# A banded-attention and gated-MLP kernel on one core: four weight sums open at once, the first batch's global queries moved to the end, values turned by VectorE and DMA

## The chip, the cores and the metric

One Trainium2 chip, one of its cores. The metric is device microseconds for one execution, median of the runs. The kernel before takes 809.63 us (three runs, 809.60 to 809.93).

## The reference

Eight batches of eight heads, 512 local and 32 global tokens each, head size 64. Global queries attend to all 544 keys; a local query attends to the 32 global keys and to local keys at most 32 positions away. The 4608 token vectors (512 wide) then go through a gated layer without a nonlinearity:

```python
s_g   = scale * q_g @ [k_g, k_l].T          # 32 x 544 per head
out_g = softmax(s_g) @ [v_g, v_l]
s_ll  = where(|i - j| <= 32, scale * q_l @ k_l.T, -1e9)
out_l = softmax([scale * q_l @ k_g.T, s_ll]) @ [v_g, v_l]
x = [out_g, out_l] as 4608 x 512
a, b = x @ w1, x @ w2                       # 512 x 1024 each
h = (a * b) @ w3                            # 1024 x 1024
result = h @ w_out                          # 1024 x 512
```

All four weight matrices arrive as 8-byte floats.

## The kernel before, in words

**Units of work.** A pair `m` (0 to 31) is two heads of one batch, four pairs to a batch; a quad `u` (0 to 15) is two pairs' global queries. A quarter `k` (0 to 16) of the gated layer takes 256 tokens: two per batch, and quarter 15 takes the 256 global tokens. The weights `w3` and `w_out` are multiplied first on the chip: the product `w34` is made in eight sums `t` of eight matmuls `fold(t, j)`, which need `w3` block (t, j // 4) and `w_out` block j. `first(k, m, c)` is 12 matmuls of x with a block of w1 (c = 0) or w2 (c = 1); `second(k, m)` multiplies the gated block with `w34` block m. Numbers are kept as a high part and a low part, so each product is three matmuls.

**A pair in steps** (names as in the order lists): loads `q`, `k`, `v`; `kc` and `vc` spread global keys and values into K and V; `s` scores on TensorE into a PSUM bank; `mm` and `ex` subtract the maximum and take exponentials, with row sums in `sm`; from pair TP = 4 on `tn` transposes blocks of 32x32 on VectorE, `po` writes them to DRAM in four DMAs and `pi` reads them back (pairs below 4 use TensorE transposes `tp` and copies `pt`); `v` values on TensorE; `iv` the reciprocal of the sums; `nm` normalizes on VectorE into `vo`; `xt` (line 396) four TensorE transposes of 128x128 into a PSUM bank; `xh` and `xl` split the result into x. K has two buffers, V three; V is filled by five DMAs a pair, since its rows are kept at three shifts.

**Global queries.** `sg` (line 427) 32 small matmuls per pair, `gm` maximum, then per quad `gr`, `ge` (exponentials), `gt` (VectorE transpose), `go` (four DMAs out), `gi` (in), `vg` values, `gn`, `gb` (one transpose), `gc`, `gd` (DMA to `xg`). At the end `gin`, `gxh`, `gxl` read `xg` for quarter 15. Each batch's global queries run beside its pairs.

**Weights.** `fetch` loads a 512 KB block into one of three raw buffers; `unit` steps 0, 2, 3 unpack it (VectorE, ScalarE, VectorE), steps 4 and 5 split a block of w1 and w2 into high and low. Blocks of w1 and w2 with m of 4 and more (`w12s`, 16 pieces of 256 KB through three buffers) are written where the blocks of `w3` and `w_out` lay, so their steps 4 and 5 wait for all eight sums and for the split of the other w1 and w2 blocks.

**Order.** Nothing is scheduled by the program: `ORDER_OF` holds, for each kind of step, its place in one global order, with a letter (A, D, P) where an engine is chosen, and each engine executes its steps in that order. SyncE (SP) issues every DMA. `ORDER` gives the order of the weight blocks, `W3F` the tiles that hold unpacked `w3` blocks. In `take(tag, bufs, ...)` a step that opens a tile waits for the readers of the tile that used the buffer before.

Of the kernel before, what the change touches and what calls it, by code (L numbers as in the profile page):

```python
# [35 lines left out]

ORDER_OF = dict(
    load="0 50 51 59 45 48 70 73 85 133 136 139 200 201 368 259 263 387 229 232 346 362 647 443 463 664 522 509 753  "
# [19 lines left out]
    "323 328 332 367 375 386 391",
    w34h="A105 D102 A155 A227 A298 A284 A359 A397",
    w34l="107 104 157 231 301 287 364 407",  # L60
    vc="A62 P65 D71 A64 A67 D75 A369 A372 P371 A377 A650 P648 P654 A660 A751 D752 P755 A754 A915 D917 P919 A918  "
    "A1016 P1015 A1018 P1020 A1183 D1185 P1187 A1186 A1284 P1283 A1286 P1288 A1451 D1453 P1455 A1454 A1552 P1551  "
    "A1554 P1556 A1719 D1721 P1723 A1722 A1820 P1819 A1822 P1824 A1987 D1989 P1991 A1990 A2088 P2087 A2090 P2092  "
    "A2252 D2254 P2256 A2255 A2345 P2346",
    kc="A72 P74 D121 A120 P186 A187 P239 P245 P322 D326 P390 P405 P500 D503 P532 A530 P705 P710 D728 P730 D807 A808  "
    "D867 P870 A960 P961 A995 P996 D1075 A1076 D1135 P1138 A1228 P1229 A1263 P1264 D1343 A1344 D1403 P1406 A1496  "
    "P1497 A1531 P1532 D1613 A1614 D1671 P1674 A1764 P1765 A1799 P1800 D1881 A1882 D1939 P1942 A2032 P2033 A2067  "
    "P2068 D2147 A2148 D2205 P2208",
    s="76 130 226 299 379 467 601 688 764 824 886 957 1032 1092 1154 1225 1300 1362 1422 1493 1568 1630 1690 1761  "
# [29 lines left out]
    iv="116 166 265 336 449 569 663 721 802 857 925 991 1067 1126 1193 1259 1335 1394 1461 1527 1603 1662 1729 1795  "
    "1873 1930 1997 2063 2139 2196 2262 2323",  # L100
    nm="160 198 294 414 499 681 733 787 834 941 988 1043 1104 1209 1256 1311 1372 1477 1524 1579 1640 1745 1792  "
    "1847 1908 2013 2060 2115 2174 2277 2320 2362",
    xt="165 203 297 419 508 682 736 794 839 942 997 1048 1109 1210 1265 1316 1377 1478 1533 1584 1645 1746 1801  "
    "1854 1913 2014 2069 2120 2179 2278 2327 2364",
# [90 lines left out]
def band_attention_glu_kernel(  # L195
# [484 lines left out]
    def pair(m):  # L680
# [74 lines left out]
        if m % 2 == 0:  # L755
            return
# [230 lines left out]
```

## Time and profile before

| | |
|---|---|
| median of 3 runs | 809.63 us |
| the profiled execution | 808.85 us, span 807.1 us |
| granted TensorE clock, mean | 0.985 |
| TensorE matmul busy | 96% of the span |
| VectorE, ScalarE, GpSimd busy | 51%, 40%, 7% |
| DMA moved | 121.30 MB, 150 GB/s |

The span runs from the first to the last instruction; the rest of the execution's time lies around it. Busy is the time in which an engine had an instruction in work. Matmuls overlap in the pipeline, so one matmul's duration is longer than the step from its start to the next one's start; costs of TensorE work are read from differences of starts. "fp32" matmuls appear as more than one record in some forms. A wait is put down to what ended it.

### The profile page before, as it was taken

Reading aid. Unit: us, or ns where it says so; the run is one execution under the profiler, and the core shown is the slowest. Engines: PE = TensorE matmul, PEld = TensorE weight load, DVE = VectorE, ACT = ScalarE, POOL = GpSimd, SP = SyncE. Lnnn points to the kernel's source line nnn. Section 1 sums busy time; section 2 is a strip of 40 time slices with the busy share of each in tenths; the row PEclk is TensorE's granted clock in tenths of the full one; section 3 lists DMA queues with packets and bytes.
Section 4 is the critical chain, followed back from the end, with each engine's and each line's share of the span. In section 5 each row is a group of like instructions: output and inputs, shape, how many; then the busy total and the mean of one; then the engine's idle time right before and its main releaser. Section 6 shows DMA issues by size and latency. Waiting matters only on the chain.

```text
span 807.1 us, 25268 instructions
## 1 busy us (share of the span) xinstructions
PE 777.9 (96%) x10676; PEld 670.9 (83%) x10676; DVE 413.0 (51%) x1333; ACT 324.0 (40%) x970; POOL 55.2 (7%) x88
## 2 busy tenths in 40 slices
PE   6699887999999999999999999999999999999998
PEld 3255486888988999998988999999899999999997
DVE  3666787756454545454554455545554645231121
ACT  3665744534343534353434334533453334111111
POOL 1000221100000100010001000100010000000000
PEclk9899999899999999999999999999999999999999
DMA  6987686477347634773375537563566353310000
GB/s 217 297 241 255 193 240 196 127 211 202 101 120 198 188 113 116 200 201 121 106 208 152 160 107 193 145 192 110 157 170 173 111 146 112 108 41 27 1 27 27
DMA packets 76489, 121.30 MB, mean 150 GB/s; under 512 B 13272, under 2 KB 41560, under 8 KB 76376
## 3 DMA queue, kind: packets, MB, share of 16 engines
q1 hardware_dynamic: 76376, 119.69, 51.1%
q8 instruction: 84, 1.38, 0.8%
q14 instruction: 29, 0.24, 0.1%
HBM read 87.15 MB, written 32.51 MB: 148 GB/s over the span
## 4 chain that ended last, share of the span: by engine, by line
PE 89%; DVE 4%; DMA 3%; ACT 2%; issue 1%; SPq 0%; DVEq 0%; ACTq 0%
PE acc L538 8%; PE bp L508 8%; PE acc L540 8%; PE acc L539 8%; PE ap L508 8%; PE bp L510 7%; PE bp L509 7%; PE ap L509 7%; PE ap L510 7%; PE w L645 5%; PE s L329 4%; PE v L379 4%; PE sg L427 2%; PE gx L462 2%; PE xt L396 2%; DMA raw_wo<-in_wo_t_dram 1%
## 5 line engine op out<-in xcount | busy, mean ns | idle before, releaser
L508 PE MATMUL bp<-x,w12h 128*128 128x256 f32 x512 | 148.4, 290 | 5.3 <-DVE gl__1520 L402 3.4
L508 PE MATMUL ap<-x,w12h 128*128 128x256 f32 x512 | 145.2, 284 | 2.5 <-DVE w12h L399 1.9
L510 PE MATMUL bp<-x,w12l 128*128 128x256 f32 x512 | 143.2, 280 | 0.9 <-issue 0.9
L510 PE MATMUL ap<-x,w12l 128*128 128x256 f32 x512 | 143.2, 280 | 0.6 <-POOL w12l L402 0.6
L509 PE MATMUL ap<-x,w12h 128*128 128x256 f32 x512 | 142.9, 279 | 0.6 <-DVE x L402 0.6
L509 PE MATMUL bp<-x,w12h 128*128 128x256 f32 x512 | 143.1, 280 | 0.0
L341 ACT ACTIVATE P<-P,mn 128x128 f32<-128x128 f32 x256 | 99.8, 392 | 27.5 <-DVE mn L336 26.7
L508 PEld LDWEIGHTS bp<-x,w12h 128*128 128x128 f32 x512 | 97.1, 190 | 10.4 <-issue 9.0
L508 PEld LDWEIGHTS ap<-x,w12h 128*128 128x128 f32 x512 | 96.7, 189 | 5.8 <-DVE w12h L399 2.1
L509 PEld LDWEIGHTS ap<-x,w12h 128*128 128x128 f32 x512 | 96.8, 189 | 3.2 <-DVE x L402 0.9
L510 PEld LDWEIGHTS bp<-x,w12l 128*128 128x128 f32 x512 | 97.7, 191 | 1.2 <-issue 1.1
L510 PEld LDWEIGHTS ap<-x,w12l 128*128 128x128 f32 x512 | 97.2, 190 | 1.2 <-POOL w12l L402 1.0
L509 PEld LDWEIGHTS bp<-x,w12h 128*128 128x128 f32 x512 | 97.4, 190 | 0.0
L336 DVE CUSTOM_DVE_ANT_0 P<-s,cs 128x128 f32<-128x128 f32 x256 | 58.8, 285 | 66.3 <-PE s L329 60.7
L645 PE MATMUL w<-wo,w3f 128*128 128x512 f32 x128 | 63.7, 635 | 10.8 <-DVE wo L569 7.5
L645 PEld LDWEIGHTS w<-wo,w3f 128*128 128x128 f32 x128 | 23.6, 199 | 40.4 <-issue 21.6
L341 ACT ACTIVATION_READ_ACCUMULATOR P<-P,mn 128x1 f32 x256 | 48.2, 188 | 0.0
L305 POOL COPY K<-K 128x480 f32<-128x480 f32 x28 | 16.8, 603 | 399.5 <-DMA K<-in_kp_t_dram 378.5
L545 ACT COPY o<-acc 128x512 f32<-128x512 f32 x34 | 20.0, 587 | 52.6 <-PE acc L540 51.1
L295 ACT COPY V<-vg 32x1024 f32<-32x1024 f32 x33 | 33.7, 1045 | 16.1 <-PE gx L465 15.9
L399 ACT CAST x<-xt 128x256 fp32r<-128x256 f32 x50 | 17.6, 373 | 55.0 <-PE xt L396 53.5
L379 PEld LDWEIGHTS v<-V,Pt 128*32 128x32 f32 x2048 | 30.2, 110 | 10.1 <-issue 4.1
(780 smaller groups left out, 1408.3 us busy)
## 6 DMA issues: line engine op xcount, KB each, us to landing
Pd<-P SPq DMA_DIRECT2D x112, 128.0 KB, 2.9
Pt<-Pd SPq DMA_DIRECT2D x28, 512.0 KB, 3.4
raw_w<-in_w_t_dram SPq DMA_DIRECT2D x24, 512.0 KB, 5.4
V<-in_v_t_dram SPq DMA_DIRECT2D x64, 192.0 KB, 4.5
K<-in_kp_t_dram SPq DMA_DIRECT2D x32, 272.0 KB, 3.2
out_dram<-o SPq DMA_DIRECT2D x34, 256.0 KB, 2.3
q<-in_q_t_dram SPq DMA_DIRECT2D x32, 256.0 KB, 3.7
V<-in_v_t_dram SPq DMA_DIRECT2D x32, 256.0 KB, 4.0
```

Of the source, the lines that this page charges most:

```text
L295: (nc.scalar.copy if eng is nc.scalar else eng.tensor_copy)(to, src)
L329: nc.tensor.matmul(block(st[:, h], x, 128 * g), q[64 * h : 64 * h + 64, c : c + 32], window(m, h, 4 * g + x), start=True, stop=True, skip_ ...
L336: nc.vector.tensor_tensor_reduce(T["P", m][:, :, h, g], chunks(T["s", m][:, h, 128 * g : 128 * g + 128]), chunks(masks[g]), -0.125, 3.0e38 ...
L341: nc.scalar.activation(P, P, AF.Exp, bias=T["mn", m][:, g, h : h + 1], scale=-1.0, accum_out=T["sm", m][:, g, h : h + 1])
L379: nc.tensor.matmul(vt[32 * x : 32 * x + 32, g, h], t[:, x, h, g], Vs[m % NV][:, x, h, g], start=True, stop=True, skip_group_check=True)
L508: nc.tensor.matmul(d, wh[:, k, c, :], x[:, 0, 0:w], start=(k == m % 2 == 0), stop=False, skip_group_check=True)
L509: nc.tensor.matmul(d, wh[:, k, c, :], x[:, 1, 0:w], start=False, stop=False, skip_group_check=True)
L510: nc.tensor.matmul(d, wl[:, k, c, :], x[:, 0, 0:w], start=False, stop=(k == 3), skip_group_check=True)
L538: nc.tensor.matmul(a, gh[:, m % 2, sl], wh, start=(m == 0), stop=False)
L539: nc.tensor.matmul(a, gh[:, m % 2, sl], wl, start=False, stop=False)
L540: nc.tensor.matmul(a, gl[:, m % 2, sl], wh, start=False, stop=(m == 7))
L645: nc.tensor.matmul(T["w34", t], T["w3f", t, j // 4][:, j % 4], T["wo"][:, j], start=(j == 0), stop=(j == 7))
```

## The change

What it does, part by part:

1. Weights: the blocks of `w3` for t = 0 to 3 come first, and four sums are open at once, two in the banks `acc` and one each in `a` and `b`. The unpacked `w3` blocks get more tiles (`x1` too, of which there are 6 in place of 7).
2. The first batch's global queries: batch 0's `sg` to `gd` leave the place beside its pairs and follow those of the last batch, as quads 16 and 17. K, V and the global values of batch 0 are loaded and spread again for them.
3. `VC` = 4: for pairs 0 to 3, V is loaded by one DMA, and four copies by an engine (`vs`) make the shifted rows.
4. Values from pair 4 on: `xt` is replaced by `vn` (VectorE transpose of 32x32 blocks), `vw` (four DMAs to DRAM) and `vi` (one DMA back into an SBUF tile `xr`, two buffers). `vo` has one buffer in place of two, `sm` two in place of three; the reciprocals go to a tile `si`. `xl` and `xh` may run on GpSimd. Tokens in x lie in another order, and `store` writes rows accordingly.
5. `sg` of two pairs in one step, so both K buffers are read by it.
6. All places in `ORDER_OF` are new.

```diff
-NX, NO, MA = (4, 7), 3, 4
+NX, NO, MA = (4, 6), 3, 4
+NXR, NVO = 2, 1
-LAG, TP = 1, 4
+LAG, TP, LATE, VC = 1, 4, 4, 4
 ORDER = (
-    ('w3', 0, 0), ('wo', 0, 0), ('w3', 1, 0), ('wo', 1, 0), ('wo', 2, 0), ('wo', 3, 0), ('w3', 0, 1), ('wo', 4, 0),
-    ('w3', 1, 1), ('wo', 5, 0), ('wo', 6, 0), ('wo', 7, 0), *[('w3', t, e) for t in range(2, 8) for e in range(2)],
+    ('w3', 0, 0), ('wo', 0, 0), ('w3', 1, 0), ('w3', 2, 0), ('w3', 3, 0), ('wo', 1, 0), ('wo', 2, 0), ('wo', 3, 0),
+    ('w3', 0, 1), ('wo', 4, 0), ('w3', 1, 1), ('w3', 2, 1), ('w3', 3, 1), ('wo', 5, 0), ('wo', 6, 0), ('wo', 7, 0),
...
-W3F = ("w3f", "w3f", "g", "as", "gh", "gl")
+W3F = ("w3f", "w3f", "g", "as", "gh", "gl", "x1", "x1", "w3f", "w3f", "g", "as", "gh", "gl", "w3f", "w3f")
+SUMS = ("acc", "acc", "a", "b", "acc", "acc", "acc", "acc")
...
         nc.sync.dma_start(V[32:64], src)
+        if m < VC:
+            return
...
+    def shift_v(m, part, eng):
+        V = Vs[m % NV]
+        if part < 2:
+            to, src = V[64 * part : 64 * part + 32, 1 - part : 4 - part], V[32:64, part : part + 3]
+        else:
+            x = 3 * (part - 2)
+            to, src = V[64 * (part - 2) :][0:32, x, :, 3 - part : 6 - part], V[32:64, 3 - x, :, part - 2 : part + 1]
+        (nc.scalar.copy if eng is nc.scalar else eng.tensor_copy)(to, src)
...
+    def values_turn(m):
+        vo = T["vo", m].rearrange("p g c d -> p c g d").rearrange("p c g d -> p (c g d)")
+        nc.vector.transpose(vo, vo)
+
+    def values_out(m):
+        vo = T.pop(("vo", m)).rearrange("p g c d -> p c (g d)")
+        d = T["vd", m] = dram.tile([128, 4, 128], F32, tag="vd", name=f"vd{m}", bufs=3)
+        for x in range(4):
+            nc.sync.dma_start(d[:, x].rearrange("(c j) q -> j c q", c=4), vo[32 * x : 32 * x + 32])
+
+    def values_in(m):
+        T["x", m] = p2.tile([128, 512], F32, tag="xr", name=f"xr{m}", bufs=NXR)
+        nc.sync.dma_start(T["x", m], T.pop(("vd", m)).rearrange("p x c -> p (x c)"))
...
-            T["w34", t] = ps_acc.tile([128, 512], F32, tag="acc", name=f"w34_{t}")
+            T["w34", t] = (ps_acc if SUMS[t] == "acc" else ps_1).tile([128, 512], F32, tag=SUMS[t], name=f"w34_{t}")
...
-        take("x", 1, ("x", m), ("xt", m))
-        add(("xt", m), "PE", [("nm", m), ("load", "cs")], back, m)
+        if m < TP:
+            take("x", 1, ("x", m), ("xt", m))
+            add(("xt", m), "PE", [("nm", m), ("load", "cs")], back, m)
+        else:
+            add(("vn", m), "DVE", [("nm", m)], values_turn, m)
+            add(("vw", m), "SP", [("vn", m)], values_out, m)
+            add(("vi", m), "SP", [("vw", m)], values_in, m)
...
-        add(("sg", m), "PE", [("load", "qg", b), *kc], g_scores, m)
+        add(("sg", u), "PE", [("load", "qg", b), *[("kc", m - x, y) for x in range(2) for y in range(2)]], g_scores, u)
...
-    for m in range(NM):
-        pair(m)
-        if m >= LAG and (m - LAG) % 2:
+    for m in range(NM + LATE):
+        if m < NM:
+            pair(m)
+        if m >= LATE:
+            global_pair(m)
+        if m >= LATE + LAG and (m - LAG) % 2:
             quad((m - LAG) // 2)
```

Some places in the two order lists of TensorE, read from `ORDER_OF` (steps between the named ones are left out at "..."):

```
before: ... fold(0,7) tp(0,0) sg(0) fold(2,0) ... fold(7,7) v(3) xt(3) first(0,0,0) first(0,1,0) first(0,0,1) first(0,1,1) first(0,2,0) sg(4) ...
after:  ... fold(4,0) ... fold(5,7) s(4) tp(3,0) tp(3,1) v(3) xt(3) first(0,0,0) first(0,1,0) fold(7,0) ... fold(7,7) first(0,0,1) first(0,1,1) ...
after:  ... v(18) first(7,1,1) second(6,6) first(7,2,0) second(6,7) first(7,3,0) v(19) ...
after:  ... sg(8) first(6,0,1) first(6,1,1) second(5,6) first(6,2,0) second(5,7) first(6,3,0) v(17) first(6,2,1) first(6,3,1) second(6,0) first(6,4,0) second(6,1) first(6,5,0) s(18) ...
```

## Rows read from the trace of the kernel before

**Rows 1.** The page's first part: busy us, share of span, instructions of each engine.

```profile
span 807.1 us, 25268 instructions
PE 777.9 (96%) x10676; PEld 670.9 (83%) x10676; DVE 413.0 (51%) x1333; ACT 324.0 (40%) x970; POOL 55.2 (7%) x88
```

**Rows 2.** Stretches: length, busy us per engine, granted clock, DMA share, GB/s.

```profile
0.00:40.00 40.00, 27.29 (x155) 13.23 (x156) 21.31 (x53) 18.32 (x37) 5.31 (x26) 0.87 0.83 257
40.00:96.00 56.00, 55.88 (x750) 29.40 (x749) 37.55 (x138) 33.50 (x97) 5.35 (x7) 1.00 0.74 228
96.00:156.00 60.00, 48.25 (x576) 41.80 (x575) 48.76 (x149) 29.56 (x98) 12.75 (x17) 0.89 0.69 196
156.00:700.00 544.00, 542.89 (x8463) 489.80 (x8466) 282.56 (x958) 225.79 (x713) 31.76 (x39) 1.00 0.54 154
700.00:803.50 103.50, 103.50 (x757) 96.70 (x745) 22.87 (x40) 16.25 (x28) 0.00 (x0) 1.00 0.07 22
```

**Rows 3.** Waits of TensorE in 0 to 160: total us, times, longest.

```profile
PE w L645 <- DVE wo L569: 7.5, 5, 3.9
PE bp L508 <- DVE gl__1520 L402: 3.4, 1, 3.4
```

**Rows 4.** Timeline of TensorE: start us, us, instruction; around one `xt`.

```profile
262.59 0.28 PE L510 MATMUL ap<-x,w12l 128*128 128x256 f32 x1
262.70 0.60 PE L396 MATMUL xt<-cs,vo 128*128 128x128 f32 x4
263.06 0.37 PE L508 MATMUL ap<-x,w12h 128*128 128x256 f32 x1
263.26 0.28 PE L509 MATMUL ap<-x,w12h 128*128 128x256 f32 x1
```

**Rows 5.** Timeline of TensorE: folds, one `sg`, two `first`, two `second`.

```profile
44.05 3.70 PE L645 MATMUL w<-wo,w3f 128*128 128x512 f32 x8
218.02 0.67 PE L427 MATMUL sg<-K,qg 64*32 64x128 f32 x32
218.62 0.51 PE L538 MATMUL acc<-w34h,gh__2651 128*128 128x512 f32 x1
222.87 0.28 PE L508 MATMUL bp<-x,w12h 128*128 128x256 f32 x1
225.59 0.39 PE L538 MATMUL acc<-w34h,gh__2851 128*128 128x512 f32 x1
228.34 0.28 PE L508 MATMUL ap<-x,w12h 128*128 128x256 f32 x1
```

**Rows 6.** Splits of the `w12s` pieces: durations ns, first and last start us.

```profile
L402 DVE TENSOR_TENSOR w12l<-raw_w12s,w12h x12: 410/425/970, 117.6 to 150.3; 128x256 fp32r<-128x256 f32 x12
```

**Rows 7.** DMA issues: count, KB each, median us to landing.

```profile
Pd<-P SPq DMA_DIRECT2D x112, 128.0 KB, 2.9
raw_w<-in_w_t_dram SPq DMA_DIRECT2D x24, 512.0 KB, 5.4
K<-in_kp_t_dram SPq DMA_DIRECT2D x32, 272.0 KB, 3.2
```

**Rows 8.** Groups by form: busy us, mean ns, idle before.

```profile
L349 DVE STREAM_TRANSPOSE P<-P 128x1024 f32<-128x1024 f32 x28 | 34.7, 1238 | 0.2
L389 DVE TENSOR_TENSOR vo<-v,sm 128x512 f32<-128x512 f32 x32 | 21.9, 683 | 11.2 <-PE v L379 11.2
L402 POOL TENSOR_TENSOR w12l<-raw_w12s,w12h 128x256 fp32r<-128x256 f32 x4 | 3.1, 775 | 6.2 <-DVE w12h L399 5.0 <-ACT w12h L399 1.0
L295 ACT COPY V<-vg 32x1024 f32<-32x1024 f32 x33 | 33.7, 1045 | 16.1 <-PE gx L465 15.9
```

**Rows 9.** Timeline of the SP queue around one pair's `po` and `pi`.

```profile
386.96 1.90 SPq L355 DMA_DIRECT2D Pd<-P  x4
391.45 0.34 SPq L360 DMA_DIRECT2D Pt<-Pd  x1
```

More of the change, by code (lines that the diff above doesn't have):

```diff
@@ L58 @@
[L58 to L69, printed above, removed]
@@ L99 @@
[L99 to L104, printed above, removed]
@@ new lines @@
+    gn="667 781 897 1036 1174 1311 1449 1587 1726 1859 1997 2135 2273 2415 2451 2480",
+    gb="677 787 901 1042 1182 1319 1455 1593 1730 1868 2003 2144 2277 2419 2454 2481",
+    gc="D681 A790 D903 D1044 A1184 A1321 D1458 D1595 D1732 D1870 D2006 D2146 D2279 D2422 A2456 D2484",
+    gd="684 795 904 1045 1186 1326 1460 1597 1734 1872 2008 2148 2281 2423 2458 2485",
+    gin="2490 2494 2499 2506",
+    gxh="D2495 D2501 D2507 D2513",
+    gxl="D2496 D2502 D2509 D2514",
+    first="391 397 433 441 444 454 460 477 499 535 514 543 599 629 606 634 637 643 651 661 679 688 702 705 714 721 732  "
[12 rows of a table added]
@@ L415, in convert, with g_scores @@
         split_x((b, p, e), f"x{e}", NX[e], T["x", m][:, 256 * e : 256 * e + 256], 256, part, eng)
-    def g_scores(m):
-        st = T["sg", m] = ps_1.tile([128, 2, 512], F32, tag="s", name=f"sg{m}")
-        u, odd = divmod(m, 2)
-        if not odd:
-            T["G", u] = p2.tile([128, 4, 4, 2, 32], F32, tag="G", name=f"G{u}", bufs=NG)
-            T["mg", u] = p2.tile([128, 4], F32, tag="mg", name=f"mg{u}")
-        for g in range(2):
-            for x in range(4):
-                for h in range(2):
-                    to = st[32 * x : 32 * x + 32, h, 0:256].rearrange("p (a b g j) -> p g a b j", a=2, b=2, g=2)[:, g]
-                    nc.tensor.matmul(to, T["qg", m // NP][64 * h : 64 * h + 64, m % NP],
-                                     window(m, h, 2 * (4 * g + x) + 1).rearrange("p a (b j) -> p a b j", b=2), start=True, stop=True, skip_group_check=True)
+    def g_scores(u):
+        st = T["sg", u] = ps_1.tile([128, 2, 512], F32, tag="s", name=f"sg{u}")
+        T["G", u] = p2.tile([128, 4, 4, 2, 32], F32, tag="G", name=f"G{u}", bufs=NG)
+        T["mg", u] = p2.tile([128, 4], F32, tag="mg", name=f"mg{u}")
+        for m in (2 * u, 2 * u + 1):
+            for g in range(2):
+                for x in range(4):
+                    for h in range(2):
+                        to = st[32 * x : 32 * x + 32, h].rearrange("p (o a b g j) -> p o g a b j", o=2, a=2, b=2, g=2)
+                        nc.tensor.matmul(to[:, m % 2, g], T["qg", m // NP][64 * h : 64 * h + 64, m % NP],
+                                         window(m, h, 2 * (4 * g + x) + 1).rearrange("p a (b j) -> p a b j", b=2),
+                                         start=True, stop=True, skip_group_check=True)
     def g_minus_max(m, h):
@@ L632, in unit @@
                 if kind == "w3" or e % 2 == 0:
-                    tag = W3F[[u[1:] for u in ORDER if u[0] == "w3"].index((a, h)) % len(W3F)]
-                    pool, n = (P["early"], 2) if tag == "w3f" else (p1, 1)
+                    tag = W3F[[u[1:] for u in ORDER if u[0] == "w3"].index((a, h))]
+                    pool, n = dict(w3f=(P["early"], 2), x1=(p1, NX[1])).get(tag, (p1, 1))
                     T["w3f", a, h] = pool.tile([128, 4, 128], F32, tag=tag, name=f"w3f{a}_{h}", bufs=n)
@@ L678, in read, with keys @@
             tiles[name].append(key)
-    def pair(m):
-        b, u = m // NP, m // 2
-        take("q", NQ, ("q", m), ("load", "q", m))
+    def keys(m):
+        b = m // NP
         take("K", NK, ("K", m), ("load", "k", m))
         take("V", NV, ("V", m), ("load", "v", m))
-        for k, fn in (("q", load_q), ("k", load_k), ("v", load_v)):
+        for k, fn in (("k", load_k), ("v", load_v)):
             add(("load", k, m), "SP", (), fn, m)
         if m % NP == 0:
-            take("qg", 2, ("qg", b), ("load", "qg", b))
-            add(("load", "qg", b), "SP", (), load_qg, b)
+            if m >= LATE:
+                take("qg", 2, ("qg", b), ("load", "qg", b))
+                add(("load", "qg", b), "SP", (), load_qg, b)
             take("vg", 4, ("vg", b), ("load", "vg", b))
@@ L696, in pair, with v_ready @@
                 late.append((("vc", m, h), tiles["V", m - NV]))
-        vc = [("vc", m, 0), ("vc", m, 1)]
+        for part in range(4 * (m < VC)):
+            add(("vs", m, part), "POOL ACT DVE", [("load", "v", m)], shift_v, m, part)
+            read(("vs", m, part), ("V", m))
         for part in range(2):
             add(("kc", m, part), "POOL ACT DVE", [("load", "k", m), ("clear", 1)], spread_k, m, part)
+    def v_ready(m):
+        return [("vc", m, 0), ("vc", m, 1), ("load", "v", m), ("clear", 2), *[("vs", m, x) for x in range(4 * (m < VC))]]
+    def pair(m):
+        b = m // NP
+        take("q", NQ, ("q", m), ("load", "q", m))
+        add(("load", "q", m), "SP", (), load_q, m)
+        keys(m)
         kc = [("kc", m, 0), ("kc", m, 1)]
@@ L702, in pair @@
         take("mn", 2, ("mn", m), ("s", m))
-        take("sm", 3, ("sm", m), ("s", m))
+        take("sm", 2, ("sm", m), ("s", m))
         take("P", 2, ("P", m), ("s", m))
@@ L728, in pair @@
         take("v", 1, ("v", m), ("v", m))
-        add(("v", m), "PE", [("pt", m, 0), ("pt", m, 1), *vc, ("load", "v", m), ("clear", 2)] if m < TP else [("pi", m), *vc, ("load", "v", m), ("clear", 2)], values, m)
+        add(("v", m), "PE", [*([("pt", m, 0), ("pt", m, 1)] if m < TP else [("pi", m)]), *v_ready(m)], values, m)
         read(("v", m), ("Pt", m), ("V", m))
         add(("iv", m), "DVE", ex, inverse, m)
-        take("vo", 2, ("vo", m), ("nm", m))
+        read(("iv", m), ("sm", m))
+        take("si", 1, ("si", m), ("iv", m))
+        read(("nm", m), ("si", m))
+        take("vo", NVO, ("vo", m), ("nm", m))
         add(("nm", m), "DVE", [("v", m), ("iv", m)], normalize, m)
-        read(("nm", m), ("v", m), ("sm", m))
-        take("x", 1, ("x", m), ("xt", m))
-        add(("xt", m), "PE", [("nm", m), ("load", "cs")], back, m)
-        read(("xt", m), ("vo", m))
+        read(("nm", m), ("v", m))
+        on = "ACT DVE POOL"
+        if m < TP:
+            take("x", 1, ("x", m), ("xt", m))
+            add(("xt", m), "PE", [("nm", m), ("load", "cs")], back, m)
+            read(("xt", m), ("vo", m))
+            on, src = "ACT DVE", ("xt", m)
+        else:
+            add(("vn", m), "DVE", [("nm", m)], values_turn, m)
+            take("vd", 3, ("vd", m), ("vw", m))
+            add(("vw", m), "SP", [("vn", m)], values_out, m)
+            read(("vw", m), ("vo", m))
+            take("xr", NXR, ("x", m), ("vi", m))
+            add(("vi", m), "SP", [("vw", m)], values_in, m)
+            read(("vi", m), ("vd", m))
+            src = ("vi", m)
         for e in range(2):
@@ L740, in pair, with global_pair @@
             take(f"x{e}", NX[e], x, ("xh", m, e))
-            add(("xh", m, e), "ACT DVE", [("xt", m)], convert, m, e, 0)
-            add(("xl", m, e), "DVE", [("xh", m, e)], convert, m, e, 1)
+            add(("xh", m, e), on, [src], convert, m, e, 0)
+            add(("xl", m, e), "DVE" if m < TP else "DVE POOL", [("xh", m, e)], convert, m, e, 1)
             read(("xh", m, e), ("x", m))
             read(("xl", m, e), ("x", m), x)
-        take("s", 1, ("sg", m), ("sg", m))
-        if m % 2 == 0:
-            take("G", NG, ("G", u), ("sg", m))
-            take("mg", 2, ("mg", u), ("sg", m))
-        add(("sg", m), "PE", [("load", "qg", b), *kc], g_scores, m)
-        read(("sg", m), ("qg", b), ("K", m))
-        for h in range(2):
-            add(("gm", m, h), "DVE", [("sg", m), ("edges",), *[("sg", m - 1)] * (m % 2)], g_minus_max, m, h)
-            read(("gm", m, h), ("sg", m))
+    def global_pair(m):
+        b, u = m // NP, m // 2
+        if m >= NM:
+            keys(m)
         if m % 2 == 0:
             return
+        take("s", 1, ("sg", u), ("sg", u))
+        take("G", NG, ("G", u), ("sg", u))
+        take("mg", 2, ("mg", u), ("sg", u))
+        add(("sg", u), "PE", [("load", "qg", b), *[("kc", m - x, y) for x in range(2) for y in range(2)]], g_scores, u)
+        read(("sg", u), ("qg", b), ("K", m - 1), ("K", m))
+        for x in range(1, -1, -1):
+            for h in range(2):
+                add(("gm", m - x, h), "DVE", [("sg", u), ("edges",)], g_minus_max, m - x, h)
+                read(("gm", m - x, h), ("sg", u))
         gm = [("gm", m - x, h) for x in range(2) for h in range(2)]
@@ L773, in quad @@
         take("x", 1, ("o", u), ("vg", u))
-        add(("vg", u), "PE", [("gi", u), ("edges",), *[(k, 2 * u + x, h) for x in range(2) for k in ("vc",) for h in range(2)],
-                              *[("load", "v", 2 * u + x) for x in range(2)]], g_values, u)
+        add(("vg", u), "PE", [("gi", u), ("edges",), *v_ready(2 * u), *v_ready(2 * u + 1)], g_values, u)
         read(("vg", u), ("Gt", u), ("V", 2 * u), ("V", 2 * u + 1), ("lg", u))
-        add(("gn", u), "DVE", [("vg", u), *([("gb", u - 1)] if u else [("warm",)])], g_normalize, u)
+        add(("gn", u), "DVE", [("vg", u), *([("gb", u - 1)] if 2 * u > LATE else [("warm",)])], g_normalize, u)
         add(("gb", u), "PE", [("gn", u)], g_back, u)
@@ L858, in weight @@
         if kind == "w3":
-            tag = W3F[[x[1:] for x in ORDER if x[0] == "w3"].index((a, e)) % len(W3F)]
-            take(tag, W3F.count(tag), ("w3f", a, e), me[3])
+            tag = W3F[[x[1:] for x in ORDER if x[0] == "w3"].index((a, e))]
+            take(tag, dict(w3f=2, x1=NX[1]).get(tag, 1), ("w3f", a, e), me[3])
         if kind[:3] == "w12":
@@ L868, in product @@
     def product(t):
-        take("acc", 2, ("w34", t), ("fold", t, 0))
+        take(SUMS[t], 2 if SUMS[t] == "acc" else 1, ("w34", t), ("fold", t, 0))
         for j in range(8):
@@ L881, in token_major @@
         take("q", NQ, ("xgr", p), ("gin", p))
-        add(("gin", p), "SP", [("gd", u) for u in range(NU)], global_in, p)
+        add(("gin", p), "SP", [("gd", u) for u in range(LATE // 2, NU + LATE // 2)], global_in, p)
         take(tag, 2, x, ("gxh", p))
```

179 lines of the change are left out of this document (97 added, 82 removed), and 121 rows, old and new, of tables (ex, first, ga, gh).

## The prediction

> **What bounds the kernel now.** I read the page's totals first, then busy time by stretch, then the waits of TensorE, then its timeline. The totals give TensorE 777.9 us of 807.1 and no other engine over 51% [rows 1]. That is an average, so the stretches decide. From 156 to 700 TensorE is busy 542.89 of 544 us, and from 700 to 803.5 all of it, at the full granted clock; VectorE is at 52%, ScalarE at 42%, DMA at 0.54 [rows 2]. There the reader is to see that only work taken from TensorE itself shortens the kernel. The first 156 us are different: TensorE stands idle 12.7 us of the first 40 and 11.75 us between 96 and 156, with the clock at 0.87 and 0.89 of full; between 40 and 96 it is busy 55.88 of 56 us [rows 2]. The idle time is 24.6 us, and at one half of full speed in part of the rest it loses up to 0.13 x 40 + 0.11 x 60 = 11.8 us more. The waits say for what: in the first stretch for unpacked weights (7.5 us for `w_out` blocks), in the second for conversions and gates on VectorE (3.4 us for one `gl`) [rows 3]. The pieces of w1 and w2 that come last are split from 117.6 to past 150.3 us, 16 of them, about one in 2.1 us [rows 6]; TensorE needs four per m.
>
> **The change, part by part.** The profiled execution took 808.85 us, 1.75 more than its span; the sum is made against it. It lies 0.78 below the median, which I add at the end.
>
> *Transposes out of TensorE.* A `first` matmul follows the one before at 0.11 us (262.59 to 262.70) [rows 4]. The four transposes of `xt` take 262.70 to 263.06, 0.36 us, and the matmul behind them needs 0.20 until the next starts, 0.09 more than usual [rows 4]: 0.45 us a pair. 28 of 32 pairs lose them: 12.5 us, all in the stretches where TensorE is full. Bounds: 28 x 0.36 = 10.1 if the switch cost stays, 28 x 0.60 = 16.8 if the whole recorded duration counted; I take 12.5, since differences of starts are what moves the next instruction.
>
> What takes their place: `vn`, a transpose of 128x512, no row; half of a 128x1024 one is 0.62 us [rows 8], bounds 0.62 and 1.24. For 28 pairs that is 17 us (at most 35) on a VectorE with 261 us free from 156 to 700 [rows 2]. `vw` and `vi` follow `po` and `pi` in form: four issues take 1.90 us of SP, the read comes 2.6 us after the last, and lands in about 3 [rows 7, 9]. So x comes some 0.6 + 1.9 + 2.6 + 3 = 8 us after `nm`, and later than before by that. For the last batch TensorE has, between v(31) and first(14,0,0), 15 steps of `first` and `second`; two `first` take 222.87 to 225.59, two `second` 225.59 to 228.34, so 1.37 each [rows 5], 20.6 us in sum. Cost 0; uncovered it would be at most 8 us per batch, 56 us. DMA carries 28 x 0.5 MB more: 14.7 MB over 544 us, 27 GB/s on 154 [rows 2]; cost 0. `xl` on GpSimd takes 0.78 us for what VectorE needed 0.42 [rows 6, 8]; nobody is near.
>
> Here a row and a rule stand against each other. `po` has the same form (blocks turned on VectorE, written by four DMAs in runs of contiguous numbers): its DMAs land in 2.9 us [rows 7], and `vw` moves half as much in runs half as long. The Trainium skill, "VectorE: DVE Perf Modes", section "The three transpose paths", warns that a plain DMA that transposes by strides is 19 times slower than the transposing DMA path. By that rule a `vw` might take 19 x 2.9 = 55 us (an estimate from that page), x would miss its cover by some 40 us in each of seven batches, and the kernel would need over 1,000 us. The row speaks against it: in `po` too the strides lie between contiguous runs, not between single numbers, and 2.9 us is what they cost.
>
> *Global scores of two pairs in one step.* The 32 matmuls of `sg` take 0.60 us (218.02 to 218.62) and about 0.11 behind them [rows 5]; the matmuls stay. In the two order lists the stretches of small matmuls without transposes are 89 before and 87 after, so about two switches of 0.2 us go: 0.4 us, which I leave out; bounds 0 and 16 x 0.2 = 3.2. The added wait is on K: both buffers are now held until `sg`, so k of the next two pairs is loaded after it. Behind sg(8) TensorE has 12 steps of 1.37 and one `v` before s(18), over 16 us; the load takes 3.2 [rows 7] and the two spreads under 2. Hidden.
>
> *One buffer for `vo`.* `nm` of the odd pair waits until `vw` of the even one has landed. Between v(18) and v(19) lie five steps, 6.9 us, and `v` itself; nm 0.68 [rows 8], vn 0.62, issues 1.9, landing 2.9 are 6.1 us. It fits with 1 to 2 us to spare. Queued behind that `nm` on VectorE are `vn` and the gate's `gb_`, which frees the bank of a later `first`. This is the thinnest cover of the change and one of the rivals.
>
> *Weights.* A 512 KB block arrives in 2.0 us at 257 GB/s [rows 2]; a fold is 3.70 / 4 = 0.93 us [rows 5]. Before, an early `w_out` block feeds two folds, 1.85 us, less than its own arrival; after, it feeds four, 3.7 us. Against that two more `w3` blocks come ahead of wo(1), each good for one fold. By arrivals (first block unpacked at about 8 us, then one per 2.0, with q, k and v of pairs 0 and 1 between) I count 24 folds and one `s` by 43 us, 23.3 us of work; counted in the same way, the order before has 20 folds and 2.6 us of small steps by then, 21.1. With the clock falling less often: 3 us gained. Bounds: -3 (the small steps that come later would have fitted) and +8 (all idle time past the first 9 us, and the clock).
>
> The second loss, 96 to 156, is 11.75 idle and up to 0.11 x 60 = 6.6 of clock. After, the eight folds of the last sum, 7.4 us, stand behind first(0,1,0), where before none was left; they are work taken from the full stretch before it, so first(0,0,0) comes earlier and the conversions run beside work. Batch 0's global queries leave this stretch too (on VectorE 8 `gm`, 2 `gr`, 2 `gt`), but four `vs` per pair come: a large one is 1.5 x 1.05 = 1.6 us by the nearest copy [rows 8], a small one about 0.5; 8 + 8 of them, 17 us, over three engines that are 10 to 81% busy there [rows 2]. V's four other DMAs of pairs 0 to 3 go, 4 x (2 x 192 + 2 x 48) KB = 1.9 MB or 8 us of the queue at 228 to 257 GB/s. I take the folds' 7.4 us as the gain. Bounds: -5 (copies delay unpacking by a third of their length) and +15. Were the folds not there as cover, the pieces' pace of 2.1 us would set the end as before: 0.
>
> *Global queries of batch 0 at the end.* Moved for quads 16 and 17: on TensorE 2 `sg`, 2 `vg`, 2 `gb`; on VectorE 8 `gm`, 2 `gr`, 2 `gt`, 2 `gn`; on ScalarE 8 `ge`; on SP 8 `go`, 2 `gi`, 2 `gd`; new are 4 k loads, 20 v loads, a qg and a vg load, 8 `kc`, 8 `vc`. TensorE's own work is unchanged; the others are at 22% and less, DMA at 0.07 after 700 [rows 2]. From sg(17) to vg(17) TensorE has 13 steps, 17.8 us, for a chain of `gm` to `gi` of about 15; from gb(17) to first(15,0,0) 11 steps, 15 us, for `gd`, `gin` and splits of about 12. Cost 0, bound 5 us if both miss.
>
> Sum: 808.85 - 12.5 - 3 - 7.4 = 785.95; with 0.78 to the median 786.7 us.
>
> **The rivals.**
> A. Only the transposes pay; at the start conversions, not the lack of work, set the pace. For it: VectorE is busy 81% of 96 to 156, and the waits there name it [rows 2, 3]. Against: TensorE is full from 40 to 96, so work moved out of there advances it. 809.63 - 12.5 = 797 us.
> B. The start nearly closes: most of the 18 us after 96 go. For it: the weights' last fetch moves ahead, since more tiles hold `w3` blocks. 809.63 - 12.5 - 5 - 14 = 778 us.
> C. Slower: `vo`'s single buffer. If `vw` lands late, the odd `nm` stands at the head of VectorE's queue, `gb_` behind it, and `first` finds its bank taken, 14 times. The gain of 22.9 us is gone at 1.64 us lost per two pairs, that is when `vw` takes 5 to 6 us longer than `po` (2 us of slack, some 2 of the gate's own). At 3 us each: 787 + 42 = 829. Against it: 2.9 us median, and 5.4 for a block four times as large under load [rows 7].
> D. The change doesn't do what it says: TensorE meets another wait of the same length in each batch, 808 us. Nothing in rows 2 shows one.
>
> **How the numbers follow.** Forecast 0.62 (its own range 781 to 792), A 0.18, B 0.12, C 0.05, D 0.02; the skill's rule of strided transposes 0.01. A measurement of this kernel tells 0.2%, 1.6 us, from no change. Forecast, A and B are faster: 0.92; D is the same: 0.02; C and the rule are slower: 0.06. The range takes in A's value with 3 us for a late tail and most of B: 777 to 800.
>
> **What would show it.** TensorE busy falls by some 15 us in total and its count by about 112 for `xt`; 156 to 790 stays at 99% or more, else C or D. Waits of TensorE before 160 sum to about 14 us instead of 24; if they stay over 22, A. `vw` should land in about 2.5 us. first(0,0,0) should come near 90 us. I am wrong if TensorE's idle time appears behind 160 us, in waits for `x`, `s` or a gate.

## The result, and the profile after

The changed kernel takes 814.88 us (median of 17 runs, 808.52 to 822.25) against 809.60 us (17 runs, 806.0 to 811.8): ratio 1.0062 with a 95% interval of 1.0041 to 1.0082, in which two executions of the changed kernel that fell in a slower state of the chip (820.71 and 822.25) are left out. It is slower, by 0.6%; the forecast was 786.7 us. The profiled execution took 811.82 us.

The totals and the stretches of the changed kernel, with the columns of [rows 1, 2]:

```profile
span 810.0 us, 25385 instructions
PE 768.9 (95%) x10564; PEld 668.7 (83%) x10564; DVE 440.9 (54%) x1371; ACT 308.2 (38%) x938; POOL 103.3 (13%) x142
```

```profile
0.00:40.00 40.00, 28.86 (x124) 13.27 (x124) 21.57 (x50) 19.03 (x34) 6.53 (x27) 0.87 0.79 250
40.00:96.00 56.00, 52.50 (x660) 30.76 (x661) 42.87 (x134) 41.60 (x111) 14.82 (x15) 0.97 0.75 223
96.00:156.00 60.00, 55.47 (x759) 47.37 (x757) 48.74 (x157) 33.17 (x106) 11.57 (x15) 0.97 0.81 223
156.00:700.00 544.00, 533.12 (x8275) 485.92 (x8274) 305.58 (x993) 198.52 (x662) 70.33 (x85) 0.99 0.65 181
700.00:803.50 103.50, 98.90 (x752) 91.40 (x750) 22.14 (x39) 15.85 (x27) 0.00 (x0) 1.00 0.11 31
```

The 112 records of `xt` are gone, as meant. TensorE's idle time before 156 fell from 24.6 us [rows 2] to 19.2. But it now stands idle 10.9 us from 156 to 700, where it was idle 1.1. (Of the 4.6 us in the last row 3.2 lie behind TensorE's end.) Its waits from 156 to the end (us in total, times, longest; one of the six for `Gt`, 1.4 us, lies behind 700):

```profile
PE gx L502 <- DMA Gt<-Gd: 8.2, 6, 2.5
PE s L349 <- POOL K L325: 3.0, 1, 3.0
PE v L399 <- DMA Pt<-Pd: 0.8, 1, 0.8
```

All of them are late transfers or stand behind one (`K`'s spread waits for the load of k). And the end of the program is strange. TensorE finishes 3.2 us earlier than before, yet the span is 2.9 us longer. This is the last issue of SP in the changed kernel (start us, us):

```profile
800.29 1.23 SPq L594 DMA_DIRECT2D out_dram<-o  x2
```

And this is what the DMA engines did from 800 to 810 us, in 40 slices of 0.25 us (tenths of 16 engines busy; GB/s):

```profile
DMA  0000002505011231222232222222232211000000
GB/s 0 0 0 0 0 16 49 33 0 25 0 16 49 66 66 57 90 98 98 98 131 98 98 98 98 98 98 98 106 123 98 82 57 41 8 0 0 0 0 0
DMA packets 264, 0.52 MB, mean 52 GB/s; under 512 B 8, under 2 KB 8, under 8 KB 264
```

The same two views of the kernel before, the second from 800 to 807.1 us:

```profile
803.50 1.02 SPq L553 DMA_DIRECT2D out_dram<-o  x2
```

```profile
DMA  0000000000000000000000005999799920000000
GB/s 0 0 0 0 0 0 0 0 0 0 0 0 0 0 0 0 0 0 0 0 0 0 0 0 219 404 381 404 289 392 404 392 70 0 0 0 0 0 0 0
DMA packets 288, 0.52 MB, mean 74 GB/s; under 512 B 32, under 2 KB 32, under 8 KB 288
```

The same 0.52 MB move at 400 GB/s with most engines busy before, and at 100 GB/s with a fifth of them after. The packets give the number: 256 carry data (2 KB each), and the small ones are read here as one per DMA and engine. 288 - 256 = 32 is two DMAs on 16 engines, 264 - 256 = 8 is two DMAs on 4. The edit behind it is the new `store`, which the section on the change names in half a sentence:

```diff
-            r = key[0] * S + 32 + 256 * key[1] + t
-            nc.sync.dma_start(out[r : r + 128], o)
+            r, x = key[0] * S + 32, 32 * (2 * key[1] + t // 128)
+            to = out[r : r + 512].rearrange("(g y) c -> g y c", g=4)[:, x : x + 32]
+            nc.sync.dma_start(to, o)
```

The first index of what is written runs over 4 groups of 32 rows, not over 128 rows. The trace of before held the price: its `store` of the global tokens runs over 4 batches in the same way. Its issue, and the DMA engines from 776 to 786 us (slices of 0.25):

```profile
776.12 1.28 SPq L555 DMA_DIRECT2D out_dram<-o  x2
```

```profile
DMA  0000015111301512222222222222222210000000
GB/s 0 0 0 0 0 33 49 8 8 8 16 16 57 123 74 98 98 98 106 98 98 107 107 98 106 90 98 98 106 106 106 82 57 8 0 0 0 0 0 0
```

### The profile page after: what moved, and what is told of

Its sections match the earlier page's. It is cut to its first block, busy times and chain, and to the rows that moved or that the text cites. A ratio compares the mean times of both kernels' runs of the same rounds, so it can differ in the third digit from the quotient of the medians.

```text
span 810.0 us, 25385 instructions
## 1 busy us (share of the span) xinstructions
PE 768.9 (95%) x10564; PEld 668.7 (83%) x10564; DVE 440.9 (54%) x1371; ACT 308.2 (38%) x938; POOL 103.3 (13%) x142
## 4 chain that ended last, share of the span: by engine, by line
PE 72%; DMA 14%; DVE 6%; SPq 3%; issue 2%; ACT 1%; POOL 1%; DVEq 0%; ACTq 0%; POOLq 0%
PE bp L548 8%; PE acc L578 7%; PE acc L579 6%; PE bp L549 6%; PE acc L580 6%; PE bp L550 6%; PE ap L548 6%; PE ap L549 6%; PE ap L550 6%; DMA Gt<-Gd 4%; PE v L399 4%; PE w L686 3%; PE s L349 3%; DMA raw_w<-in_w_t_dram 2%; PE gx L502 2%; DMA K<-in_kp_t_dram 2%
## 5 line engine op out<-in xcount | busy, mean ns | idle before, releaser
L548 PE MATMUL bp<-x,w12h 128*128 128x256 f32 x512 | 151.7, 296 | 1.2 <-DVE gl__1361 L442 0.8
L549 PE MATMUL bp<-x,w12h 128*128 128x256 f32 x512 | 144.2, 282 | 0.0
L686 PE MATMUL w<-wo,w3f 128*128 128x512 f32 x128 | 63.0, 631 | 10.7 <-DVE wo L610 6.7
L315 POOL COPY V<-vg 32x1024 f32<-32x1024 f32 x40 | 44.7, 1138 | 172.0 <-PE gx L505 143.3
L325 POOL COPY K<-K 128x480 f32<-128x480 f32 x40 | 24.4, 616 | 173.4 <-DMA K<-in_kp_t_dram 144.6
L490 ACT ACTIVATE G<-G,mg 128x256 f32<-128x256 f32 x64 | 32.0, 501 | 34.9 <-DVE mg L484 17.5
L349 PE MATMUL s<-K,q 64*32 64x128 f32 x2048 | 38.0, 277 | 3.3 <-POOL K L325 3.0
L399 PE MATMUL v<-V,Pt 128*32 128x64 f32 x2048 | 36.2, 223 | 4.9 <-DMA Pt<-Pd 2.9
```

The costliest lines, as they stand in the source:

```text
L315: (nc.scalar.copy if eng is nc.scalar else eng.tensor_copy)(to, src)
L349: nc.tensor.matmul(block(st[:, h], x, 128 * g), q[64 * h : 64 * h + 64, c : c + 32], window(m, h, 4 * g + x), start=True, stop=True, skip_ ...
L399: nc.tensor.matmul(vt[32 * x : 32 * x + 32, g, h], t[:, x, h, g], Vs[m % NV][:, x, h, g], start=True, stop=True, skip_group_check=True)
L548: nc.tensor.matmul(d, wh[:, k, c, :], x[:, 0, 0:w], start=(k == m % 2 == 0), stop=False, skip_group_check=True)
L549: nc.tensor.matmul(d, wh[:, k, c, :], x[:, 1, 0:w], start=False, stop=False, skip_group_check=True)
L686: nc.tensor.matmul(T["w34", t], T["w3f", t, j // 4][:, j % 4], T["wo"][:, j], start=(j == 0), stop=(j == 7))
```

## The experiments

Theory S: the pattern of `store` holds four of the 16 DMA engines for some 8 us, 16 times (two stores each), and every later transfer that needs all 16 waits for those four. Rival T: it costs only the tail, and the new waits come from the other parts of the change.

**1. Four DMAs of 32 rows (a_four).**

```diff
-            nc.sync.dma_start(to, o)
+            for g in range(4):
+                nc.sync.dma_start(to[g], o[32 * g : 32 * g + 32])
```

> The changed kernel with each `store` of a batch's tokens sent as four DMAs of 32 rows instead of one whose first index runs over 4 groups; the rows are the same. Theory S (the store pattern keeps each store on 3 or 4 of the 16 DMA engines, at 100 GB/s): the last two stores land in about 2.5 us instead of 9, so the tail alone gives 6 us; in the middle the waits for `Gt`, `Pt` and K shrink because no DMA engine is held for 9 us: of the 11 us idle between 156 and 700 about 8 go, and TensorE's pace stays. 812 - 6 - 8 = about 798 us, ratio to before 0.985. Rival T (only the tail): 806, ratio 0.995, with the vg waits at 8 us in sum as now. Rival N (SP's queue pays for three more issues per store, 32 x 2 x 3 issues): no gain, 812 or more.

Measured: 798.19 us, ratio 0.986 [0.9832, 0.9888]. The waits for `Gt` are gone and TensorE is busy 542.58 of 544 us from 156 to 700: S, not T. At the end 384 packets move instead of 264: 256 with data and 128 small, eight DMAs on 16 engines each.

**2. One DMA to 128 consecutive rows (a_line).** `to = out[r + 4 * x : r + 4 * x + 128]`.

> The changed kernel with each `store` as one DMA to 128 consecutive rows (the rows of a batch land in another order; this part of the result is changed). It takes the pattern away without any further issue. Theory S: as with four DMAs or 1 us better, 797 us; rival T 806; if four DMAs are slower than this by over 2 us, issues on SP's queue have a price.

Measured: 790.81 us, ratio 0.9777 [0.9759, 0.9794]. S again. The four DMAs are slower than one by 7 us. Of that the profiled executions show 2.8 (spans 791.4 and 788.6), most of it at the end, where eight issues take 3.62 us instead of 1.03.

**3. The pattern alone, on the kernel before (b_group).** Its `store` gets the three lines marked + above.

> The kernel before with the changed kernel's `store` pattern alone (4 groups of 32 rows; the rows of a batch land in another order, which changes this part of the result). Theory S: the tail grows by 6 to 7 us and waits for DMAs appear behind 156 us; 816 to 820 us, ratio 1.008 to 1.013. Rival T: the tail alone, 815.5 to 816.5, with idle time between 156 and 700 at 1 us as before. If the ratio is 1.00, the pattern costs nothing and the tail of the changed kernel has another cause.

Measured: 832.31 us, ratio 1.0278 [1.0257, 1.03]: 23 us slower, over twice what even S expected. From 156 to 700 this kernel shows the stretch and the first wait that follow, in place of 542.89 us busy [rows 2]:

```profile
156.00:700.00 544.00, 530.00 (x8171) 477.72 (x8171) 277.39 (x950) 221.86 (x707) 30.82 (x38) 0.99 0.53 150
```

```profile
PE v L379 <- DMA Pt<-Pd: 10.7, 5, 2.4
```

Here the victim is `Pt`, in the changed kernel `Gt`: a transfer that comes behind the store with little slack. The first long wait, on SP's queue and on TensorE, in this kernel:

```profile
252.28 1.29 SPq L554 DMA_DIRECT2D out_dram<-o  x2
253.75 0.43 SPq L360 DMA_DIRECT2D Pt<-Pd  x1
263.23 0.98 PE L379 MATMUL v<-V,Pt 128*32 128x64 f32 x55 [2.18 <-DMA Pt<-Pd]
```

and the same place in the kernel before, where nothing waits:

```profile
250.10 1.03 SPq L553 DMA_DIRECT2D out_dram<-o  x2
251.31 0.33 SPq L360 DMA_DIRECT2D Pt<-Pd  x1
258.79 0.93 PE L379 MATMUL v<-V,Pt 128*32 128x64 f32 x51
```

`Pt` is issued right behind the store in both. The wait for it ends 9.5 us after the issue here; in the kernel before TensorE starts 7.5 us after it without a wait, and the recorded landings of `Pt` take 3.1 to 4.9 us. That the transfer waits for just the four engines which the store holds fits this, but the traces don't name an engine.

**4. The transposes alone (b_noxt).** In the kernel before, `back` returns `vo` itself from pair 4 on.

> The kernel before with the transposes `xt` of 28 pairs left out (conversions read `vo` unturned; this part of the result is changed). It measures the first term of the sum by itself. The sum's 0.45 us a pair: 12.5 us less, 797 us, ratio 0.985. If only the matmuls' own time goes (0.36): 799.5. If TensorE's pace between 156 and 700 is set by something else than its own work, less than 8 us.

Measured: 795.63 us, ratio 0.9832 [0.981, 0.9853]: 13.8 us in the medians and in the spans (807.1 and 793.3), 0.49 a pair.

**5. The order of tokens put right at the split (a_order).**

```diff
+        src = T["x", m].rearrange("p (x g q) -> p g x q", x=4, g=4)[:, 2 * e : 2 * e + 2]
...
-            hi_of(X[key][:, 0, 0:w], src, eng)
+            hi_of(tokens(X[key][:, 0, 0:w]), src, eng)
...
+    def tokens(ap):
+        return ap.rearrange("p (g x q) -> p g x q", g=2, x=4)
```

`lo_of` likewise; `store` is that of before.

> The changed kernel with the order of tokens put right where `x` is split instead of at the `store`: `xh` and `xl` read `x` as (g, x, q) and write tokens in order, so a `store` is one DMA to 128 consecutive rows, as before. Theory S (all of the loss was the store pattern): the time of the kernel with consecutive rows, 790 to 792 us, ratio 0.977. Rival P (reading in runs of 32 numbers makes the splits slower than the plain ones): splits over 0.6 us instead of 0.42 and 0.78, x late, 795 or more.

Measured: 790.34 us, ratio 0.9763 [0.9736, 0.979]. The splits on VectorE take 442 ns (`xl`) and 323 (`xh`), against 436 and 322 in a_eight, which reads `x` plainly: reading in runs of 32 costs 6 ns and 1 ns, and rival P falls. This kernel has all parts of the change; it is faster than a_four and level with a_line. Its stretches up to the last store, and then the landing of its stores:

```profile
0.00:40.00 40.00, 29.60 (x123) 13.48 (x123) 19.94 (x44) 17.55 (x28) 6.29 (x27) 0.83 0.79 245
40.00:96.00 56.00, 52.71 (x660) 30.64 (x661) 44.35 (x142) 43.24 (x118) 13.75 (x15) 0.97 0.73 226
96.00:156.00 60.00, 55.87 (x759) 47.65 (x758) 48.84 (x157) 33.35 (x106) 11.51 (x15) 0.97 0.80 224
156.00:700.00 544.00, 543.17 (x8438) 495.56 (x8437) 307.59 (x1001) 200.98 (x667) 69.81 (x85) 1.00 0.66 184
700.00:784.20 84.20, 84.20 (x590) 78.14 (x588) 18.48 (x31) 12.88 (x22) 0.00 (x0) 1.00 0.07 20
```

```profile
out_dram<-o SPq DMA_DIRECT2D x34, 256.0 KB, 2.6
```

How the store reaches `Gt` is seen on SP's queue around one of them, first in the changed kernel, then in a_order (start us, us of issuing):

```profile
285.57 1.28 SPq L594 DMA_DIRECT2D out_dram<-o  x2
288.00 4.13 SPq L375 DMA_DIRECT2D Gd<-G  x4
292.25 3.16 SPq L432 DMA_DIRECT2D vd<-vo  x4
295.84 0.34 SPq L380 DMA_DIRECT2D Gt<-Gd  x1
```

```profile
281.20 1.02 SPq L597 DMA_DIRECT2D out_dram<-o  x2
283.63 3.08 SPq L375 DMA_DIRECT2D Gd<-G  x4
286.81 1.84 SPq L432 DMA_DIRECT2D vd<-vo  x4
288.82 0.34 SPq L380 DMA_DIRECT2D Gt<-Gd  x1
```

From the store to the issue of `Gt` are 10.3 us in the one and 7.6 in the other, with the same issues between; those of `Gd` and `vd` themselves take 2.4 us longer. Landings are not recorded for the changed kernel, but the ends of TensorE's waits bound them: five of its six waits for `Gt` end 5.0 to 7.7 us after the issue of `Gt` (the one behind the rows above 3.9), where a_order's recorded landings take 3.4 to 4.9. So the store delays what follows it twice: SP issues more slowly, and what it issues lands later, as `Pt` in b_group.

**6. Eight groups of 16 rows (a_eight).** `rearrange("(g y) c -> g y c", g=8)[:, y : y + 16]`.

> The changed kernel with each `store` written as 8 groups of 16 rows instead of 4 groups of 32 (rows of a batch land in another order, which changes this part of the result). Theory S4 (the first index of the written pattern sets how many DMA engines a store uses: 4 before, 8 now): the last two stores leave 256 + 2 x 8 = 272 packets instead of 264, DMA share 0.4 to 0.5 and some 200 GB/s, the tail is 2.5 us shorter, and the waits in the middle fall by more than half: 796 to 804 us, ratio 0.983 to 0.993. Rival G (gaps between the groups cost, however many groups there are): 812 to 818, 100 GB/s as now or less.

Measured: 795.39 us, ratio 0.9839 [0.9805, 0.9872], as S4 said; G falls, since there are more gaps and it is faster. From 784 to 791.7 us (slices of 0.19):

```profile
DMA  0000000000000467215245455455554300000000
GB/s 0 0 0 0 0 0 0 0 0 0 0 0 0 106 74 53 21 11 64 96 181 192 181 202 213 170 213 202 192 202 192 128 32 0 0 0 0 0 0 0
DMA packets 272, 0.52 MB, mean 68 GB/s; under 512 B 16, under 2 KB 16, under 8 KB 272
```

16 small packets, 8 engines a DMA, 200 GB/s: twice the engines, twice the rate.

**7. `second` in pairs (a_pairs), 8. no pad (a_pad0), 9. both (a_best).** All three on a_order. In 47 places of TensorE's list second(m), first, second(m+1) becomes second(m), second(m+1), first; `PAD = (48, 0)` becomes `(0, 0)`.

> As a_order, and in 47 places TensorE's order second(m), first, second(m+1) becomes second(m), second(m+1), first, which is how the kernel before has it. Theory W: the single buffers `gh` and `gl` are read until the later `second` ends, so a split pair makes `gl` late and with it the bank of the next `bp`; 40 or so starts of `bp` that come 0.1 to 0.2 us late go, 2 to 5 us less than a_order: 786 to 789. Rival: these starts are late for another reason, 791; or the gate behind is later by as much and the time grows.

> As a_order, with the 48 unused numbers per partition at the head of the pool `p1` taken away, so that its tiles (x, as, g, gh, gl) lie 192 bytes lower. A `first` matmul follows the next at 114 ns (even k) and 116 ns (odd k) in the kernel before and at 117 and 115 ns in the changed one, whatever the store. Theory A (where x lies in SBUF sets it): the intervals change, by 1 to 3 ns either way, and the time by 2 to 9 us of 3072 x 1 to 3 ns. Rival: the intervals stay at 117 and 115 and the time at that of a_order within 1.5 us; then placement by so little is not the cause.

> a_pairs and a_pad0 together: store of consecutive rows, `second` in pairs, no pad. If both small gains are real and add: 788 to 788.5, ratio 0.974. If the two are within what a measurement tells: 789 to 790.

Measured, in this order: 788.89 us, ratio 0.975 [0.9717, 0.9782]; 789.76, 0.976 [0.9734, 0.9786]; 788.36, 0.9737 [0.9713, 0.9761]. All overlap with a_order's interval, so no gain over it is shown. What the traces show is the step between two `first` matmuls, the mean over the even and the odd k from 4 to 13: 116.8 and 115.4 ns in a_order, 115.8 and 116.3 without the pad, 114.1 and 115.7 before. Without the 192 bytes the odd k are the slower ones, and the sum stays. But a_pairs, which has the pad, shows 115.8 and 115.2: the order moves this step too, and what sets it is not shown. Theory W has only the profiled executions for it: spans of 785.1 and 788.1, and over the last eight gates, where no attention runs, a_order falls back by 0.9 us against the kernel before and a_pairs by none. The medians don't decide.

**10. V's parts by DMA again (a_vc0)**, a_order with `VC = 0`.

> As a_order, with the `vs` copies of pairs 0 to 3 left out and V's neighbour parts brought by DMA again, as before (1.9 MB more in the first 150 us, 16 copies fewer). Theory Q (at the start the SP queue and the weights behind it set the pace): the weights come later by 4 to 8 us and the kernel loses 2 to 6 us: 792 to 796. Theory E (VectorE, ScalarE and GpSimd set the pace there, and the copies delay the unpacking): 1 to 4 us faster, 786 to 789. If within 1.5 us of a_order, that part of the change neither pays nor costs.

Measured: 798.31 us, ratio 0.9853 [0.9825, 0.9881]: 8 us lost, more than Q asked. VectorE's waits for arriving blocks in the first 100 us, first a_order, then a_vc0 (whose profiled execution, 801.14 us, was the slowest of its six):

```profile
DVE raw_w L609 <- DMA raw_w<-in_w_t_dram: 14.2, 7, 6.8
```

```profile
DVE raw_w L609 <- DMA raw_w<-in_w_t_dram: 21.6, 8, 6.9
DVE raw_wo L609 <- DMA raw_wo<-in_wo_t_dram: 7.1, 4, 4.2
```

**11. V's copies alone, on the kernel before (b_vs).** `shift_v` and `if m < 4: return` in `load_v`, with 16 places for `vs` in its order.

> The kernel before with the changed kernel's `vs` copies alone: V's neighbour parts of pairs 0 to 3 are copied on chip, 1.9 MB of DMA in the start stage goes; weights' order, `store` and all else as before. Leaving them out of the mended kernel cost 8 us. Theory V (the queue's 8 us set the start by themselves): 6 to 8 us faster, 802 to 804, ratio 0.990 to 0.993. Theory C (they pay only together with the new order of the weights and the later global queries, which make work out of weights that come sooner): 0 to 2 us, ratio 0.998 to 1.000. Theory E (VectorE is the bound at the start, 81% of 96 to 156): slower, ratio above 1.001.

Measured: 815.37 us, ratio 1.0082 [1.0057, 1.0107]: slower by 6.7 us, as theory E said. From 40 to 96 us DMA moved 188 GB/s instead of 228 [rows 2]. Some 18 of these 40 GB/s are the parts of V that this run leaves out (two pairs' in this stretch, 1.0 MB); for the rest, the queue waits for tiles that the engines empty later (this stretch; then SP's costliest wait in the first 100 us, a wait that sums to 9.9 us in the kernel before):

```profile
40.00:96.00 56.00, 53.99 (x586) 27.49 (x593) 35.92 (x130) 35.15 (x98) 3.75 (x5) 0.97 0.58 188
```

```profile
SPq L621 <- DVE w3f L581: 20.6, 7, 11.2
```

The same copies are worth 8 us in the one order and cost 7 in the other, as I placed them; their price can't be told apart from the order.

**12. Four DMAs with consecutive rows, on the kernel before (b_four).** `for x in range(0, 128, 32): nc.sync.dma_start(out[r + x : r + x + 32], o[x : x + 32])`.

> The kernel before, same rows, each `store` sent as four DMAs of 32 consecutive rows instead of one of 128. It prices three more issues per store, without gaps in the rows, on the kernel whose own store is fast. If only SP's issue time counts: the last two stores are issued over 3.6 us instead of 1.0, +2.5 us, ratio 1.003. If more DMAs in the queue also cost in the middle (the changed kernel with four DMAs took 798, with one DMA 790): +7, ratio 1.008 to 1.010.

Measured: 811.16 us, ratio 1.0018 [1.0, 1.0036]. More issues cost 1.3 us in the medians here, with an interval from none to 2.9 us. Why four DMAs cost the changed kernel 8 us against one (798.19 and 790.34) stays open: its profiled execution (793.15) was the fastest of its six and shows only 3.3 us of it.

## Why the prediction was wrong

The step that failed: every edit of the change was to be costed, and the new `store` was not. The change section says that "`store` writes rows accordingly"; the sum has no term for it, and what it says of DMA is bytes alone ("27 GB/s on 154 ...; cost 0"). Bytes were not the matter. The measured term is 16.0 us up to TensorE's end and 5.9 behind it (changed kernel and a_order, profiled executions), 24 us in the medians. It is nearly the whole miss: with the store mended and all else as changed the kernel takes 790.34 us, inside the forecast's own range of 781 to 792.

This table, worked out from the timelines of TensorE, shows where each kernel stands to the one before: the start of the first `second` of gate n (68 gates, four to each half batch), in us less than (-) or over before.

```
gate   before   changed   a_order   b_group   b_noxt
  4     173.4    -11.5     -11.3      +1.2     -0.5
 14     279.8     -9.2     -13.5      +4.4     -3.2
 30     447.6     -9.5     -17.8      +8.3     -8.2
 46     614.1    -10.1     -21.0     +16.0    -12.0
 56     714.4     -7.4     -21.3     +18.0    -13.8
 67     800.6     -3.2     -19.2     +18.4    -13.8
```

At gate 4 the changed kernel has its start's gain, the same as a_order. (3.4 us of it are TensorE's own `sg` and `vg`: less of them stands ahead of this gate, since batch 0's come last.) Then it gains nothing more: at the next gates of the table it is 4.3, 8.3, 10.9, 13.9 and 16.0 us behind a_order, and so loses to the stores about what b_noxt saves on `xt`. Last comes the tail.

By the prediction's own steps:

- *Transposes, 12.5:* right, 13.8 (b_noxt, a run by itself, within the bounds of 10.1 and 16.8). `vn` took 711 ns, `vw` landed in 2.6 us in a_order, and `x` was in time.
- *Start, 3 and 7.4:* half right. TensorE's idle time in the three stretches is 10.4, 3.3 and 4.1 us in a_order, against 12.7, 0.1 and 11.75 [rows 2]: 2.3 and 7.6 less where the sum looked, 3.2 more between 40 and 96, which it took for full whatever was moved out of it. The 8 us of queue that V's DMAs leave free were set against the copies and counted for nothing; by a_vc0 the start's gain needs them: without the copies gate 4 comes no earlier than before, in the one execution profiled.
- *`vo`, K, the global queries last, 0:* right. Once the store is mended TensorE waits 0.8 us behind 156, and no `nm` for `vd`.
- *Global scores in one step, left out:* the steps of the `sg` matmuls, each from its start to the next start without idle time, sum to 17.5 us in a_order and 19.3 before; 1.8 us gained, within the bounds of 0 and 3.2.
- *Not foreseen, +3.2:* a `first` follows the one before at 116.2 ns in a_order and 115.2 before (mean from k = 2 on), on 3264 of them. `second` went the other way: between gates 4 and 56 the steps of its 624 matmuls, each to whatever follows it, sum to 145.2 us in a_order and 150.8 before, those of `first` to 303.4 and 296.8. The two nearly cancel, and the cause of neither is shown.
- *Rivals:* D had the right form ("another wait of the same length in each batch"), and was put at 0.02 because rows 2 show no such wait; but those rows show only the old store. C's wait never came. Idle time behind 160 us, the forecast's own sign of being wrong, did come, but most of it for `Gt`, which it had not named.

The rule that bore on this change was not the one weighed. The prediction took up the 19-fold price that the Trainium skill, "VectorE: DVE Perf Modes", section "The three transpose paths", puts on a plain DMA that transposes by strides, against the transposing path, where the innermost stride of what it writes is large. Multiplying `po`'s 2.9 us by it was a wrong base, since `po` is itself a plain DMA. `vw` writes runs of 128 numbers and landed in 2.6 us; no run here transposes by strides between single numbers, so the price itself was not tried. The Trainium skill, "DMA: Bandwidth & Descriptors", section "Why a DMA increments its semaphore by 16 and not by 1", says that a DMA uses the largest number of engines up to 16 that divides the slowest dimension of both its sides. By that rule 4 groups give 4 engines, 8 give 8 and 128 rows give 16; the packets of the three kernels, 264, 272 and 288, agree.

## What to carry to other kernels

Read each DMA's access pattern as a number of engines, not only as bytes: the same 256 KB took a quarter of the engines because the first index ran over 4. When an edit changes a pattern, look in the old trace for a transfer of the same form and read its rate; here one stood at 776 us. And where data come in another order, turn them round in an instruction that runs anyway: the splits did it for next to nothing, where the store cost 24 us.

## What the hardware showed that was not expected

- A DMA on four engines slows the others: with b_group's pattern as the only edit, the waits for `Pt` rose to 10.7 us, a `Pt` issued behind a store ended its wait 9.5 us after the issue, and the whole kernel lost 23 us, of which 5.8 are its tail (9.4 us from the last store's issue to the end, 3.6 before).
- Issuing itself grew: four `vd` took 3.16 us on SP behind such a store, 1.84 without; from 156 to 700 a DMA took SP 541 ns on average in the changed kernel and 498 in a_order. In b_group the mean is 501 against 491 before, so there the loss shows in the landings.
- Steps between `first` matmuls differ by 1 to 3 ns between the even and the odd k and between the kernels; with 48 floats of pad taken away the other k were the slower ones, in one profiled execution each.
